# A linear-attention and FFN kernel: another order of the first steps, other filler products, later second halves of the attention output

## The chip, the cores and the metric

One core of one Trainium2 chip runs the whole program. The metric is the device time of one execution in microseconds (us); lower is better. TensorE is called PE here (PEld is its loading of the stationary operand), VectorE DVE, ScalarE ACT, GpSimd POOL; SyncE (SP) only issues DMAs.

## The reference: what is computed

Two stages, all in fp32 (the FFN's weights arrive in a wider format and are converted on the chip):

```python
for t in range(S):        # batch 4, heads 8, S = 768, head size 48
    state = alpha[:, :, t, :, None] * state + einsum('bhd,bhe->bhde', k[:, :, t], v[:, :, t])
    y[:, :, t] = einsum('bhd,bhde->bhe', q[:, :, t], state)
x = y.transpose(0, 2, 1, 3).reshape(3072, 384)
h = maximum(x @ w_in, 0)          # w_in 384 x 2048
out = (h * h) @ w_out             # w_out 2048 x 384
```

So every token gets a gated linear-attention output, and the outputs of all heads, side by side, go through a feed-forward network with a squared ReLU.

## The kernel before, in words

**Blocks.** The sequence of each batch is cut into six chunks of 128 tokens; a block is one chunk of one batch with all eight heads, so there are 24 blocks, numbered so that blocks 0 to 3 are the first chunks of the four batches. The state goes from block n to block n + 4.

**One block.** `load` (L130) brings alpha ("a"), q, k and v. `ln` takes the logarithm of alpha on ACT (L261); `cs` sums it along the tokens by one product with a triangle of ones on PE (L283, two PE rows); `eb` and `ei` take the exponential of the sum and of its negative on ACT (L294, L298); `mq` and `mk` scale q and k by them on DVE (L302). `qT` and `kT` turn them on PE (L354, four transposes each), `qc` and `kc` copy the results out of PSUM (L368). `sc` forms the scores (L413) and `kv` the sums of k times v (L442), 32 PE rows each. `am` masks the scores on DVE (L424), `us` adds the old state (L456), `lt` turns the last row of the decay (L337, copied out by ACT as "last", L344), and `st` makes the next state (L477, L479).

**A pair of blocks.** The output y is formed for two blocks together. `ga` (L502) does the scores and sums of the block n coming next, then the state's part and the first half of y for the pair a before it; `gb` (L524) does the second half of y (the other halves of the masked scores, L393) and then the scores and sums of block n + 1. The two halves are apart because one writes other rows of the PSUM banks than the other. `ev` (L596; `ep` in the written order, L616) copies y out of PSUM into x, the FFN's transposed input, in up to twelve pieces on ACT or DVE.

**The FFN.** Blocks go through it in groups of four: 24 blocks are six groups (0 to 5). `ffn_in` (L909) does it plainly for group 0, one of 16 columns blocks j at a time: three products (two PE rows each), the ReLU on ACT (L925) and the square on ACT (L928). The first four j are done in halves of 256 tokens (`ha`, `hb`), since the first pair's x is there before the second's. From group 1 on each fp32 product is split into three of a rounded type (`in_x`, `in_y`, L726; `out_x`, `out_y`, L809), whose parts DVE and ACT make (L653, L648, L701).

**Weights.** `weights` (L146) loads a slab, one eighth of w_in or w_out; `first` (L169) converts half of its bits on ACT (two rows, L179), `second` (L184) does the rest on DVE (four rows, L192 to L199).

**What sets the order.** The program is recorded under a manual schedule: each engine runs its instructions in the order written. Three things write it. (1) The prelude: `AT["pre"]` names the first loads, then fills (memsets), masks and a few products of zeros (`warm`, L236) are issued. (2) For blocks 0 to 3 a string, `AT["first"]`, is a list of words (step name and block), run one after the other. (3) After that `attention` (L1006) puts the same steps at planned times ("FFN steps", one being one unit of FFN work) and `weave` (L1051) mixes them with the FFN's units; `AT["ga"]` and `AT["gb"]` are the times of `ga` and `gb` after an attention pair's start.

**Loads.** All DMAs stand in one queue on SP in the order of issue. `move` (L108) makes a load wait until an earlier one has landed, about three loads back, so that the queue isn't filled far ahead:

```python
for before, took in reversed(under_way):
    if ahead >= AT["thrp" if us == 1.0 else "thr"]:
        tc.add_manual_dep(ins, before.name, ...)
        break
    ahead += took
```

**Names the prediction uses.** "Sums 2" is `cs2`, "scores 2" `sc2`, "log 2" `ln2`, and so on with the block's number; "slab 0" is the first eighth of w_in; a PE "row" is one line of the trace's records, of which an fp32 product has two.

Of the kernel before, what the change touches and what calls it, by code (L numbers as in the profile page):

```python
# [9 lines left out]
FP32 = mybir.dt.float32  # L10
FP32R = mybir.dt.float32r
# [4 lines left out]
AF = mybir.ActivationFunctionType  # L16
ALU = mybir.AluOpType
# [1 line left out]


GB = 4
AT = {'thrp': 4.5, 'cvo': 3.35, 'thr': 2.25, 'm48': 16, 'cvs': 3.9, 'cv1': 0.125, 'later': (0, 0, 4, 6, 0, 1, 0), 'evs': 0.1, 'lead': 4, 'post': 3, 'w_first': (46.0, 38.0, 49.0), 'wstep': 1.0, 'w_in_at': 2.5, 'w_in_by': 3.6, 'room1': 22, 'room': 24, 's0': 4, 'ahead': 6, 'late': 2, 'xs': 0.0, 'g0': ((0.5, 4, False, True, 27.75), (25.75, 6, True, True), (29.25, 8, True, False)), 'sc0': (3.25, 2.35, 2.35), 'g1': ((5.5, 8, False, 15.0), (13.0, 10, True), (35.25, 12, True)), 'g': ((2.075, 6, True), (14.25, 8, True)), 'g1x': 51.0, 'gx': 48.75, 'g0x': 56.25, 'k0': 2, 'h0': 15, 'k1': 4, 'h1': 3, 'h1by': 2, 'evs0': 0.7, 'tp': 'ADMD', 'tp1': 'ADAD', 'split': 8, 'o0': (46.5, 48.5), 'o1': (), 'o2': (21.25, 24.75, 24.5, 40.0, 35.25, 28.25), 'str1': 21.5, 'ga': 9.75, 'gb': 12.5, 'cv0': -1.25, 'pre': '1a 0a 0q 0k 1k 1q', 'cp': ('q2a', 'k2b', 'k0a', 'k3a', 'k3b', 'k0b', 'q0b', 'q3b', 'q2b', 'q3a'), 'evd': ((0, 0, 0), (0, 0, 1), (0, 1, 2), (0, 1, 3), (2, 0, 3), (2, 1, 1), (2, 1, 2)), 'first': 'ln0 load1v cs0 ei0 eb0 zeros4 mk0 mq0 qT0 kT0 ln1 cs1 kc0 ei1 warm0 load0v eb1 mk1 qc0 weights0 lt1 sc0 load2a mq1 load2q kT1 kc1 qT1 load2k load3a qc1 load3k kv0 am0 first0 load3v sc1 ln2 kv1 load3q us0 am1 weights6 us1 cs2 ya0 ei2 second0 eb2 lt0 ln3 yb0 load2v mq2 qT2 mk2 load4a ep00 ep01 qc2 kT2 cs3 kc2 eb3 ei3 zeros1 sc2 ep02 mq3 mk3 kT3 ep03 weights2 first1 st0 ha0 second1 lt2 kv2 am2 qT3 load4k kc3 qc3 ha1 weights5 first2 sc3 kv3 am3 load4q us2 ha2 us3 ya2 yb2 weights3 ep20 ep21 ep22 load4v ep23 second2 first3 weights1 st1 weights4 ha3 lt3 hb0 st2 second3 hb2 hb3 hb1 st3'}


RUN = {0: 128, 32: 32, 64: 64, 96: 32}
# [3 lines left out]
def kernel(  # L29
# [12 lines left out]
    nc = tc.nc  # L42
    B, H, S, D = q.shape
    C = 128
    NCH = S // C
    NP = H // 2
# [24 lines left out]
    s_t = [s_all.pop(0) for _ in range(B)]  # L71
    NV = 4
# [4 lines left out]
    for t in tiles["q"] + tiles["k"]:  # L77
        nc.gpsimd.memset(t[:, :, D:64], 0.0)

    NW = 8  # L80
    wt_pool = ctx.enter_context(tc.tile_pool(name="wt", bufs=26))
# [15 lines left out]
    lent = {("a", n): flat(wt("a_lent"))[:, 0 : H * D] for n in (2, 3)}  # L97
    for x, n in (("q", 2), ("q", 3), ("k", 3)):
        t = lent[x, n] = two_k("qk_lent", shape=(H, 64))
        nc.gpsimd.memset(t[:, :, D:64], 0.0)  # L100

    def tile_of(x, n):
        return lent.get((x, n), tiles[x][n % len(tiles[x])])
# [4 lines left out]
    def move(us, out, in_):  # L108
        ins = nc.sync.dma_start(out=out, in_=in_).ins
# [90 lines left out]

    for word in AT["pre"].split():
        load(int(word[0]), word[1:])
# [12 lines left out]
    ident = consts.tile([128, 128], FP32, name="ident")  # L215
    make_identity(nc, ident)
    causal = cv_pool.tile([128, C], FP32, tag="upper", name="causal")
    make_upper_triangular(nc, causal, 1.0, diag=True)
    causal_r = consts.tile([128, C], FP32R, name="causal_r")
    nc.gpsimd.tensor_copy(out=causal_r, in_=causal)  # L220
# [4 lines left out]
    for t in s_all + u_all:  # L225
# [10 lines left out]
    def warm(_):  # L236
        nc.tensor.matmul(
            out=ps_att.tile([128, NP, 64], FP32, tag="att", name="warm"),
            lhsT=s_t[0].rearrange("a p d -> a (p d)")[:, 0:128], rhs=s_t[0], start=True, stop=True,
        )  # L240

    for _ in range(3):
        warm(0)


# [18 lines left out]

    SPLIT = AT["split"]

# [106 lines left out]
    def kc(n):  # L373
        (copied if n < GB else turned_copied)("k", n)


    def zeros(n):

# [85 lines left out]
    def rows_of(n):  # L464
        return [slice(0, D), slice(64, 64 + D)] if n >= AT["m48"] else [slice(0, 128)]

# [174 lines left out]
    here, todo, room = {}, [], [22]  # L641
# [8 lines left out]
    late = [False]  # L650
# [83 lines left out]
    def in_x(j):  # L734
        acc["h", j] = ps_ffn.tile([128, GB * C], FP32, tag="att", name="h")
        in_passes(j, "b", "a", True, False)
        in_passes(j, "l", "l", False, True)
        x = acc["h", j]
        if kinds[0][j % 4] == "D":
            hid[j] = two_k("hid")  # L740
            nc.scalar.activation(out=hid[j], in_=x, func=AF.Copy, scale=E)  # L741
        else:
            nc.scalar.activation(out=x, in_=x, func=AF.Copy, scale=1.0 + E)  # L743

    def in_y(j):
        given.add(("hy", j))
        in_passes(j, "d", "d", False, True)
        if kinds[0][j % 4] == "D":
            combine(((hid[j], acc.pop(("h", j)), ALU.add, hid[j]),))

    kinds = [""]

    def in_post(j):
        need(("hy", j))
        given.add(("h", j))
        if kinds[0][j % 4] == "D":
# [7 lines left out]
        if kinds[0][j % 4] == "M":  # L764
# [144 lines left out]
    def ffn_in(g, j, cols=slice(0, GB * C)):  # L909
        need(("w", j * NW // NJ))  # L910
        if cols.start == 0:
            need(("x", 0))
        if cols.stop == GB * C:
            need(("x", 2))
        w, c0 = w_in[j * NW // NJ], j % (NJ // NW) * 128
        n = cols.stop - cols.start
        ps = ps_ffn.tile([128, GB * C], FP32, tag="att", name="h")[:, 0:n]
        for kk in range(KM):
            nc.tensor.matmul(  # L919
                out=ps, lhsT=w[:, kk, c0 : c0 + 128], rhs=xT[g][kk][:, cols],  # L920
                start=(kk == 0), stop=(kk == KM - 1),
            )
# [31 lines left out]
    steps = {f.__name__: f for f in (ln, sp, cs, eb, ei, mq, mk, bl, br, lt, qT, qc, kT, kc, ev)}  # L954
# [11 lines left out]

    steps["ep"] = ep
    steps["zeros"] = zeros

    def half_in(x, j):  # L970
        given.add(("h" + x, j))
# [5 lines left out]
    first = AT["first"]  # L977
    for word in first.split():
        f = max((x for x in steps if word.startswith(x)), key=len)
        rest = word[len(f) :]  # L980
        steps[f](*([int(rest[0]), rest[1:]] if f == "load" else map(int, rest)))


    PLAN = (
# [122 lines left out]
    cv0 = AT["cv0"]  # L1107
    cvs = AT["cvs"]
# [17 lines left out]
    for g in range(1, NG):  # L1126
# [11 lines left out]
        if g == 1:  # L1138
# [5 lines left out]
            n = min(AT["k0"], AT["k1"])  # L1144
# [34 lines left out]
```

## Time and profile before

| | |
|---|---|
| median of 3 runs | 518.98 us (518.58 to 520.09) |
| span of the profiled execution | 518.6 us |
| time of the profiled execution itself | the page gives its span alone |
| PE busy | 507.8 us (98%) |
| DVE busy | 355.7 us (69%) |
| ACT busy | 306.4 us (59%) |
| DMA moved | 102.34 MB, 197 GB/s in the mean |
| products of h in group 0 (L919) | 128x512: 0.43 us from start to start |

A busy PE is counted from an instruction's start to its modelled end, and products overlap, so what counts is the time from one start to the next. A line of the timeline gives start, length, engine, source line, operation, output and inputs, the number of instructions merged and, in brackets, how long the engine stood idle before and what ended that. The chain of waits goes backwards from the last instruction: at each step to what released it. The granted clock is 1.00 in all five-microsecond stretches up to 45 us.

### The profile page before, as it was taken

The numbers are of one execution on the slowest core, as the hardware profiler recorded it, in microseconds if no ns is written. First come the engines' busy times: TensorE is split into PE (matmuls) and PEld (weight loads), VectorE is DVE, ScalarE is ACT, GpSimd is POOL, SyncE is SP. The second block draws the span as 40 slices with busy tenths as digits, with TensorE's granted clock in tenths as the row PEclk, the third lists the DMA queues.
The fourth block names the chain that finished last, engine by engine and source line by source line (L and its number), as shares of the span: only waits on it lengthen the run. The fifth ranks groups of instructions, "written<-read, shape, count | busy, mean of one in ns | idle before, by whom it ended". The sixth has DMA issues, their size and how long they took to land.

```text
span 518.6 us, 13019 instructions
## 1 busy us (share of the span) xinstructions
PE 507.8 (98%) x5338; PEld 418.9 (81%) x5338; DVE 355.7 (69%) x628; ACT 306.4 (59%) x649; POOL 5.3 (1%) x29
## 2 busy tenths in 40 slices
PE   7899999999999999999999999999999999999997
PEld 5675455678888669987899988899988899988997
DVE  2766669986887877776697468587465487363861
ACT  4788898547888653485664276772275673164620
POOL 4000000000000000000000000000000000000000
PEclk9999999999999999999999999999999999999999
DMA  9999779472777786898884688864683545699201
GB/s 183 204 267 237 197 189 235 93 228 80 238 190 184 246 243 162 265 279 227 205 225 143 222 247 222 223 200 152 213 274 124 185 121 154 207 380 322 65 2 61
DMA packets 139323, 102.34 MB, mean 197 GB/s; under 512 B 109808, under 2 KB 115968, under 8 KB 139264
## 3 DMA queue, kind: packets, MB, share of 16 engines
q1 hardware_dynamic: 139264, 101.51, 68.2%
q8 instruction: 42, 0.69, 0.6%
q14 instruction: 17, 0.14, 0.1%
HBM read 84.16 MB, written 17.33 MB: 196 GB/s over the span
## 4 chain that ended last, share of the span: by engine, by line
PE 93%; DVE 4%; issue 1%; POOL 1%; ACT 1%; DVEq 0%; POOLq 0%
PE o L809 39%; PE h L726 32%; PE h L919 8%; PE y L393 4%; PE sckv L413 2%; PE T L578 2%; PE sckv L442 2%; PE cs L283 1%; PE cs L286 1%; DVE x L616 1%; PE cs L287 1%; DVE hd L648 1%; DVE hx L653 0%; DVE am L424 0%; ACT x L616 0%
## 5 line engine op out<-in xcount | busy, mean ns | idle before, releaser
L726 PE MATMUL h<-xd,wd 128*128 128x512 f32 x240 | 68.1, 396 | 1.1 <-issue 1.1
L726 PE MATMUL h<-xa,wb 128*128 128x512 f32 x240 | 68.7, 394 | 0.0
L726 PE MATMUL h<-xl,wl 128*128 128x512 f32 x240 | 67.9, 391 | 0.0
L648 DVE TENSOR_TENSOR hid<-h,hid 128x512 f32<-128x512 f32 x40 | 27.6, 689 | 51.1 <-PE h L726 51.0
L616 ACT COPY x<-y 48x256 f32<-48x256 f32 (+3 forms) x133 | 46.7, 365 | 21.2 <-PE y L393 18.8
L809 PE MATMUL o<-wb,ha 128*128 128x384 f32 x160 | 54.5, 340 | 0.0
L743 ACT ACTIVATE h<-h 128x512 f32<-128x512 f32 x40 | 23.3, 582 | 52.3 <-PE h L726 52.3
L809 PE MATMUL o<-wl,hl 128*128 128x384 f32 x160 | 53.7, 336 | 0.1
L809 PE MATMUL o<-wd,hd 128*128 128x384 f32 x304 | 53.7, 334 | 0.0
L809 PE MATMUL o<-w_out,hid 128*128 128x384 f32 x160 | 53.6, 489 | 0.0
L726 PEld LDWEIGHTS h<-xl,wl 128*128 128x128 f32 x240 | 45.1, 188 | 10.1 <-DVE xl L653 0.4
L809 PEld LDWEIGHTS o<-wd,hd 128*128 128x128 f32 x304 | 52.8, 188 | 0.0
L726 PEld LDWEIGHTS h<-xa,wb 128*128 128x128 f32 x240 | 44.4, 188 | 9.8 <-ACT hid L763 0.4
L726 PEld LDWEIGHTS h<-xd,wd 128*128 128x128 f32 x240 | 44.0, 188 | 9.1
L809 PE MATMUL o<-wb,hx 128*128 128x384 f32 x144 | 48.3, 336 | 0.0
L809 PE MATMUL o<-wl,hx 128*128 128x384 f32 x144 | 48.1, 334 | 0.0
L809 PEld LDWEIGHTS o<-w_out,hid 128*128 128x128 f32 x160 | 30.0, 190 | 19.7
L741 ACT ACTIVATE hid<-h 128x512 f32<-128x512 f32 x40 | 24.2, 606 | 32.9 <-PE h L726 32.5
L919 PE MATMUL h<-x,w_in 128*128 128x512 f32 (+1 forms) x120 | 43.4, 512 | 0.2 <-DVE x L616 0.2
L701 ACT ACTIVATE ha<-hid 128x512 fp32r<-128x512 f32 x40 | 25.1, 642 | 20.3 <-PE o L809 7.9
L919 PEld LDWEIGHTS h<-x,w_in 128*128 128x128 f32 x120 | 22.1, 190 | 17.8 <-issue 15.3
L653 DVE SCALAR_TENSOR_TENSOR hl<-ha,hid 128x512 fp32r<-128x512 f32 x40 | 27.5, 687 | 6.9 <-ACT ha L701 6.8
(111 smaller groups left out, 852.5 us busy)
## 6 DMA issues: line engine op xcount, KB each, us to landing
wd<-do SPq DMA_DIRECT2D x36, 384.0 KB
wl<-lo SPq DMA_DIRECT2D x34, 384.0 KB
wl<-li SPq DMA_DIRECT2D x32, 384.0 KB
wd<-di SPq DMA_DIRECT2D x32, 384.0 KB
raw<-in_moe_w_out_dram SPq DMA_DIRECT2D x8, 767.5 KB
raw<-in_moe_w_in_dram SPq DMA_DIRECT2D x8, 767.2 KB
v_in<-in_v_dram SPq DMA_DIRECT2D x24, 192.0 KB
out_dram<-osb SPq DMA_DIRECT2D x24, 192.0 KB
```

What stands on the lines that cost most here:

```text
L393: ins = nc.tensor.matmul(out=ys[e][64 * half : 64 * half + D + G * e, m % 2, p // 2, t], lhsT=lhsT, rhs=rhs, start=(half, e) not in seen, ...
L413: nc.tensor.matmul(out=ps[e][HALF[h], 0, p, :], lhsT=ks[rows, p, HALF[h]], rhs=qs[rows, p, HALF[h]], start=True, stop=True, skip_group_che ...
L442: nc.tensor.matmul(out=ps[h][64 * e : 64 * e + m, 1, p, G:64], lhsT=tile_of("k", n)[HALF[h], 2 * p + e, 0:m], rhs=tiles["v"][n % NV][HALF[ ...
L616: copy(out=x[kk][to : to + m, t : t + 2], in_=blk[n]["y"][e][r : r + m, :, p // 2],)
L648: nc.vector.tensor_tensor(out=o, in0=x, in1=z, op=op)
L653: nc.vector.scalar_tensor_tensor(out=o, in0=x, scalar=c, in1=y, op0=ALU.mult, op1=op)
L701: nc.scalar.activation(out=a, in_=x, func=AF.Copy, scale=NEAR * E)
L726: nc.tensor.matmul(out=acc["h", j], lhsT=here[w, "i", p][:, kk, jj * 128 : (jj + 1) * 128], rhs=x_parts[x][:, kk], start=start and kk == 0 ...
L741: nc.scalar.activation(out=hid[j], in_=x, func=AF.Copy, scale=E)
L743: nc.scalar.activation(out=x, in_=x, func=AF.Copy, scale=1.0 + E)
L809: nc.tensor.matmul(out=acc[t][:, 0:DM], lhsT=lhs[:, t * C : (t + 1) * C], rhs=rhs, start=start, stop=stop, skip_group_check=True,)
L919: nc.tensor.matmul(out=ps, lhsT=w[:, kk, c0 : c0 + 128], rhs=xT[g][kk][:, cols], start=(kk == 0), stop=(kk == KM - 1),)
```

## The change

It touches tables and the prelude; the FFN from group 1 on is the same work.

- The first loads and their order: k of block 1 comes third, ahead of q and k of block 0. In the written order the first slab of weights goes ahead of both v loads, alpha of block 3 goes ahead of k and q of block 2, the second slab goes ahead of k3, v3 and v2.
- POOL makes the triangle of ones first; DVE fills the padding of the q and k tiles, which POOL did; the states s0 to s2 are filled later.
- Products of zeros: two of 512 columns at the start instead of three of 256; in the written order one product of 128 columns at two places, instead of four of 128, one of 256 and one of 128.
- The words of `AT["first"]` are in another order: the sums of block 1 directly behind those of block 0; the copies of k1, k2 and q1 out of PSUM on DVE (before, the names in `AT["cp"]` matched no block and all copies were on ACT); other pieces of x on DVE (`evd`).
- Squares of `ffn_in` named in `AT["hv"]` are done on DVE: four of 256 columns and that of j = 4 with 512.
- `AT["gb"]` goes from 12.5 to 14.0, so that in the planned part the second half of a pair's y, the copies into x, the scores of the pair's second block and three loads come 1.5 FFN steps later.

```diff
-AT = {... 'gb': 12.5, 'pre': '1a 0a 0q 0k 1k 1q',
- 'cp': ('q2a', 'k2b', 'k0a', 'k3a', ...),
- 'evd': ((0,0,0), (0,0,1), (0,1,2), (0,1,3), (2,0,3), (2,1,1), (2,1,2)),
- 'first': 'ln0 load1v cs0 ei0 eb0 zeros4 mk0 mq0 qT0 kT0 ln1 cs1 kc0 ei1 warm0 load0v eb1 mk1 qc0
-  weights0 lt1 sc0 load2a mq1 load2q kT1 kc1 qT1 load2k load3a qc1 load3k kv0 am0 first0 load3v sc1
-  ln2 kv1 load3q us0 am1 weights6 us1 cs2 ya0 ei2 second0 eb2 lt0 ln3 yb0 load2v mq2 qT2 mk2 load4a
-  ep00 ep01 qc2 kT2 cs3 kc2 eb3 ei3 zeros1 sc2 ep02 mq3 mk3 kT3 ep03 weights2 first1 st0 ha0 second1 ...'}
+AT = {'warms': 0, 'wides': 2, 'hv': ((1,256), (2,256), (3,0), (3,256), (4,0), (4,256)),
+ ... 'gb': 14.0, 'pre': '1a 0a 1k 0q 0k 1q', 'cp': ('k1', 'k2', 'q1'),
+ 'evd': ((0,0,0), (0,0,1), (0,0,3), (2,0,0), (2,0,1), (2,1,3)),
+ 'first': 'ln0 cs0 ln1 cs1 weights1 load0v ei0 eb0 mq0 load1v load2a ei1 qT0 zeros1 mk1 load3a mk0
+  kT0 eb1 kT1 mq1 qc0 load2k kc0 sc0 load2q first0 lt1 qT1 kc1 am0 kv0 qc1 us0 ln2 sc1 kv1 load3q
+  cs2 am1 us1 eb2 ei2 ln3 lt0 weights6 load3k second0 ya0 yb0 cs3 load3v mq2 mk2 ep00 load2v weights0
+  eb3 mq3 ep01 ei3 kT2 kc2 qT2 load4a qc2 zeros1 ep02 st0 qT3 ep03 sc2 mk3 first1 ha0 kT3 am2 ...'}
...
-    for t in s_all[0:B]:
-        nc.gpsimd.memset(t, 0.0)
     s_t = [s_all.pop(0) for _ in range(B)]
+    nc.gpsimd.memset(s_t[3], 0.0)
+    causal = ...; make_upper_triangular(...); causal_r = ...; ident = ...
...
+    for t in pads:
+        nc.vector.memset(t[:, :, D:64], 0.0)
...
-    for _ in range(3):
+    for _ in range(AT["wides"]):
+        nc.tensor.matmul(
+            out=ps_att.tile([128, 2 * NP, 64], FP32, tag="att", name="warm"),
+            lhsT=s_t[3].rearrange("a p d -> a (p d)")[:, 0:128],
+            rhs=s_t[3][:, 0:1, :].to_broadcast([128, 2 * NP, 64]), start=True, stop=True,
+        )
+    for _ in range(AT["warms"]):
         warm(0)
...
-        nc.scalar.activation(out=hid[j][:, cols], in_=r, func=AF.Square)
+        if (j, cols.start) in AT["hv"]:
+            nc.vector.tensor_tensor(out=hid[j][:, cols], in0=r, in1=r, op=ALU.mult)
+        else:
+            nc.scalar.activation(out=hid[j][:, cols], in_=r, func=AF.Square)
```

More of the change, by code (lines that the diff above doesn't have):

```diff
@@ new lines @@
+AT = {'warms': 0, 'wides': 2, 'hv': ((1, 256), (2, 256), (3, 0), (3, 256), (4, 0), (4, 256)), 'thrp': 4.5, 'cvo': 3.35, 'thr': 2.25, 'm48': 16, 'cvs': 3.9, 'cv1': 0.125, 'later': (0, 0, 4, 6, 0, 1, 0), 'evs': 0.1, 'lead': 4, 'post': 3, 'w_first': (46.0, 38.0, 49.0), 'wstep': 1.0, 'w_in_at': 2.5, 'w_in_by': 3.6, 'room1': 22, 'room': 24, 's0': 4, 'ahead': 6, 'late': 2, 'xs': 0.0, 'g0': ((0.5, 4, False, True, 27.75), (25.75, 6, True, True), (29.25, 8, True, False)), 'sc0': (3.25, 2.35, 2.35), 'g1': ((5.5, 8, False, 15.0), (13.0, 10, True), (35.25, 12, True)), 'g': ((2.075, 6, True), (14.25, 8, True)), 'g1x': 51.0, 'gx': 48.75, 'g0x': 56.25, 'k0': 2, 'h0': 15, 'k1': 4, 'h1': 3, 'h1by': 2, 'evs0': 0.7, 'tp': 'ADMD', 'tp1': 'ADAD', 'split': 8, 'o0': (46.5, 48.5), 'o1': (), 'o2': (21.25, 24.75, 24.5, 40.0, 35.25, 28.25), 'str1': 21.5, 'ga': 9.75, 'gb': 14.0, 'cv0': -1.25, 'pre': '1a 0a 1k 0q 0k 1q', 'cp': ('k1', 'k2', 'q1'), 'evd': ((0, 0, 0), (0, 0, 1), (0, 0, 3), (2, 0, 0), (2, 0, 1), (2, 1, 3)), 'first': 'ln0 cs0 ln1 cs1 weights1 load0v ei0 eb0 mq0 load1v load2a ei1 qT0 zeros1 mk1 load3a mk0 kT0 eb1 kT1 mq1 qc0 load2k kc0 sc0 load2q first0 lt1 qT1 kc1 am0 kv0 qc1 us0 ln2 sc1 kv1 load3q cs2 am1 us1 eb2 ei2 ln3 lt0 weights6 load3k second0 ya0 yb0 cs3 load3v mq2 mk2 ep00 load2v weights0 eb3 mq3 ep01 ei3 kT2 kc2 qT2 load4a qc2 zeros1 ep02 st0 qT3 ep03 sc2 mk3 first1 ha0 kT3 am2 kc3 second1 qc3 ha1 weights5 lt3 kv2 us2 load4k sc3 kv3 first2 ha2 am3 weights4 us3 st1 ya2 load4v yb2 ep20 ep21 lt2 weights3 ep22 ep23 ha3 second2 st3 hb2 first3 hb3 hb0 second3 hb1 load4q st2 weights2'}
@@ L68 @@
     u_all = kept("us", 3, [128, NP, 64])
-    for t in s_all[0:B]:
-        nc.gpsimd.memset(t, 0.0)
     s_t = [s_all.pop(0) for _ in range(B)]
+    nc.gpsimd.memset(s_t[3], 0.0)
+    causal = cv_pool.tile([128, C], FP32, tag="upper", name="causal")
+    make_upper_triangular(nc, causal, 1.0, diag=True)
+    causal_r = consts.tile([128, C], FP32R, name="causal_r")
+    nc.gpsimd.tensor_copy(out=causal_r, in_=causal)
+    ident = consts.tile([128, 128], FP32, name="ident")
+    make_identity(nc, ident)
     NV = 4
@@ L76 @@
     }
-    for t in tiles["q"] + tiles["k"]:
-        nc.gpsimd.memset(t[:, :, D:64], 0.0)
+    pads = tiles["q"] + tiles["k"]
     NW = 8
@@ L99 @@
         t = lent[x, n] = two_k("qk_lent", shape=(H, 64))
-        nc.gpsimd.memset(t[:, :, D:64], 0.0)
+        pads.append(t)
     def tile_of(x, n):
@@ L214 @@
     nc.scalar.preload_act_table_set("natural_log_exp_and_others")
[L215 to L220, printed above, removed]
     halves_mask = consts.tile([128, C // 2], FP32, name="halves_mask")
@@ L224 @@
         nc.gpsimd.tensor_copy(out=halves_mask[rows], in_=causal[rows, rows])
-    for t in s_all + u_all:
+    for t in s_t[0:3] + u_all + s_all:
         nc.gpsimd.memset(t, 0.0)
@@ L238, in warm @@
             out=ps_att.tile([128, NP, 64], FP32, tag="att", name="warm"),
-            lhsT=s_t[0].rearrange("a p d -> a (p d)")[:, 0:128], rhs=s_t[0], start=True, stop=True,
+            lhsT=s_t[3].rearrange("a p d -> a (p d)")[:, 0:128], rhs=s_t[3], start=True, stop=True,
         )
-    for _ in range(3):
+    for _ in range(AT["wides"]):
[5 more added lines that the diff above has]
+    for _ in range(AT["warms"]):
         warm(0)
@@ L374, in kc, with wide, tiny @@
         (copied if n < GB else turned_copied)("k", n)
+    def wide(n):
+        ps = bank(n, "zeros", (2 * NP, 64))
+        for _ in range(n):
+            nc.tensor.matmul(
+                out=ps, lhsT=s_t[3].rearrange("a p d -> a (p d)")[:, 0:128],
+                rhs=s_t[3][:, 0:1, :].to_broadcast([128, 2 * NP, 64]), start=True, stop=True,
+            )
+    def tiny(n):
+        ps = bank(n, "zeros", (2 * NP, 64))
+        for _ in range(n):
+            nc.tensor.matmul(
+                out=ps[0:8, 0, 0:1], lhsT=s_t[3][:, 0, 0:8], rhs=s_t[3][:, 0, 0:1],
+                start=True, stop=True,
+            )
     def zeros(n):
@@ L738, in in_x @@
         x = acc["h", j]
-        if kinds[0][j % 4] == "D":
+        if kinds[0][j % len(kinds[0])] == "D":
             hid[j] = two_k("hid")
@@ L755, in in_post @@
         given.add(("h", j))
-        if kinds[0][j % 4] == "D":
+        if kinds[0][j % len(kinds[0])] == "D":
             h = hid[j]
@@ L968 @@
     steps["zeros"] = zeros
+    steps["tiny"] = tiny
+    steps["wide"] = wide
     def half_in(x, j):
@@ L980 @@
         rest = word[len(f) :]
-        steps[f](*([int(rest[0]), rest[1:]] if f == "load" else map(int, rest)))
+        steps[f](*([int(rest[0]), rest[1:]] if f == "load" else [int(rest)] if f in ("zeros", "tiny", "wide") else map(int, rest)))
     PLAN = (
```

5 lines of the change are left out of this document (2 added, 3 removed).

## The prediction

> **What bounds the kernel now.** I read the busy tenths of the span first, then five-microsecond stretches, then the waits and the timeline of the first 40 us. The tenths come first.
>
> ```profile
> PE   7899999999999999999999999999999999999997
> DVE  2766669986887877776697468587465487363861
> ACT  4788898547888653485664276772275673164620
> ```
>
> PE has slack only in the first two slices (0 to 26 us) and in the last. By stretches:
>
> ```profile
> 5.00:10.00 5.00, 4.33 (x15) 3.53 (x16) 1.03 (x2) 1.80 (x4) 1.19 (x6) 1.00 1.32 186
> ...
> 15.00:20.00 5.00, 3.90 (x169) 3.15 (x173) 4.67 (x10) 3.30 (x7) 0.00 (x0) 1.00 0.84 165
> 20.00:25.00 5.00, 3.64 (x73) 2.92 (x64) 4.83 (x12) 4.47 (x12) 0.00 (x0) 1.00 1.01 263
> ...
> 40.00:45.00 5.00, 5.00 (x17) 2.91 (x16) 4.69 (x10) 2.62 (x8) 0.00 (x0) 1.00 0.99 245
> ```
>
> After the length come busy PE, PEld, DVE, ACT, POOL, then clock, DMA share, GB/s. From 40 us PE is full, so what the change does early is worth as many us as it brings forward the moment from which PE never waits again. The chain of waits in time order has that moment:
>
> ```profile
> 36.10 0.42 DVE x L616
> 36.52 0.03 issue
> 36.55 0.44 DVE x L616
> 36.99 0.04 issue
> 37.04 8.02 PE h L919 x28
> ```
>
> The last copy into the first group's x ends at 36.99; the FFN's products start at 37.04 and run through. Where the time before that goes:
>
> ```profile
> 8.56 0.41 SPq L109 DMA_DIRECT2D raw<-in_moe_w_in_dram  x1
> 11.19 0.37 SPq L109 DMA_DIRECT2D a_lent<-in_alpha_dram  x1
> ...
> 16.67 0.53 ACT L261 ACTIVATE a_lent<-a_lent 128x384 f32<-128x384 f32 x1
> ...
> 20.11 0.52 ACT L261 ACTIVATE a_lent<-a_lent 128x384 f32<-128x384 f32 x1
> ```
>
> ACT takes the logarithm of block 2 only at 16.67, behind the conversion of the first weight slab (14.88 to 16.79), and that of block 3 at 20.11, behind the second copy of "last". Their cumulative sums follow at 17.25 and 21.66 on PE.
>
> **When the loads land.** The loads are one queue. I summed GB/s over half-microsecond stretches and took 0.197 MB for a load and 0.786 MB for a slab (192.0 and 767.2 KB in the page's last part): alpha of block 0 is complete at 4.0, the eighth load at 10.2, the first slab at 12.9, the second goes from 20.7 to 23.4. So a load takes 1.03 us and a slab 2.7. The log of block 0 starts at 5.04 and the load that waits for v0 issues at 11.19, so a landing is about 1.0 behind its bytes. In the new queue order (alpha 1, alpha 0, k1, q0, k0, q1, slab 0, v0, v1, alpha 2, alpha 3, k2, q2, q3, slab 1, k3, v3, v2, slab 2) that gives landings, as estimates from these rows: q1 9.2, slab 0 11.9, v0 12.9, v1 13.9, alpha 2 15.0, alpha 3 16.0, k2 17.0, q2 18.1, q3 19.1, slab 1 21.8, k3 22.8, v3 23.9, v2 24.9, slab 2 27.6. The other end: from 13.7 to 18.0 the queue of before needs 1.43 us for each of three loads (133 and 86 GB/s in 15 to 17), and its third slab takes 3.2. With 1.43 from v0 to q2 and 3.2 for slabs, k3 lands at 26 and v2 at 28.
>
> **The change, part by part.**
>
> *Products of zeros and fills.* Three products of 256 columns become two of 512 (four PE rows at 0.86 instead of six at 0.43: 1.10 to 4.6 instead of 3.7); four of 128 (1.71 us, 7.28 to 8.99) and one of 256 go; one of 128 is added before block 0's k transpose, at most 0.43. POOL makes the mask first (causal_r done near 2.0 instead of 4.29) and DVE fills the pads (eight of about 0.2, over before 5). Worth nothing: the first sums wait for ACT's log at 5.04 to 5.56, which waits for alpha 0, and that load keeps its place. Without this cover it would cost the 0.86 that PE runs longer.
>
> *Blocks 0 and 1.* The sums of block 1 go ahead of block 0's transposes, so its exponentials end near 9.5 instead of 12.06. But block 0's values now come after the slab, 12.9 instead of 11.2. Even with every product at the slow spacing (0.73 for half a sum), block 1's second transpose ends by 13.2 and its copy, now on DVE, by 13.9. That copy from PSUM has no DVE row: between 0.42 (256 columns) and 0.79 (a masked copy of 2x256) I take 0.65, nearest to 0.69 of the 512-column sum that reads PSUM. So this is a loss hidden by the next wait: sc1 13.95, kv1 to 15.05.
>
> *Block 2 and 3 gates.* Slab 0 lands at 11.9, ACT converts it to 13.85 (1.91), copies "last" to 14.2, and takes log 2 at its landing, 15.0. Sums 2 run at 15.6 against 17.25; the y products of blocks 0 and 1 at 16.7 to 18.6 against 18.09 to 20.3; log 3 comes ahead of "last" at 17.2 and sums 3 run at 18.6 against 21.66. This is the gain: 1.65 at y, 3.0 at sums 3.
>
> *Where part of it is given back.* DVE is full here (4.67 and 4.83 of 5). Converting slab 0 takes it 15.8 to 18.75 (2.93, as in 17.18 to 20.11); then q2, k2 (0.55 each), a copy of x 0.42, q3 0.55 to 20.8, two copies, the copy of k2's transpose (0.65, new on DVE) to 22.2. So scores 2 start at 22.25 against 22.80: only 0.55 left. Then the state (0.72), two copies of x, k3 to 24.3. PE: first half-width FFN unit 22.9 to 24.4 (its last third waits for x), k3 transposes 25.0, second unit 26.4, "last" of block 3 0.45, kv2 27.3, scores 3 (copies ready 26.7) 27.95, kv3 28.4, third unit 29.9 (its weights 28.0), y of blocks 2 and 3 to 31.7 against 33.75. The x copies there took 33.75 to 36.99, 3.24; the new split is as long. End near 35.0: **2.0 earlier**. With late loads the same walk has k3 scaled at 26.6, kv2 at 29.5, y to 33.9, end 37.2: **0.2 later**. The 1.03 row holds for most loads, so I take 1.7.
>
> *Squares moved to DVE* (four of 256 columns, 0.42 each on ACT, and one of 512, 0.63): after 35 us PE is full with four half units (1.46 each) and needs the third slab's weights only behind these, near 41; DVE has them at about 38.7. Nothing; if later than 41, what is missing.
>
> *Second half of y 1.5 steps later.* No work changes: 8 to 16 o products or nine h products (1.4 to 2.8 us) go ahead of it. The tightest place is the end of group 1: y moves from 204.1 to 206.9, its twelve ACT copies (4.37) end at 211.9 instead of 209.2, the three splits' first parts at 213.6, the DVE parts at 214.5; PE wants them at 214.08 to 215.2, each in time by 0.3 or more. The v and k loads move with it and have 8 steps left. One stall may go or come:
>
> ```profile
> 237.35 0.62 PE L726 MATMUL h<-xd,wd 128*128 128x512 f32 x2
> 239.08 0.40 PE L726 MATMUL h<-xd,wd 128*128 128x512 f32 x1 [1.11 <-issue]
> ```
>
> It stands between two dense bursts of attention rows and waits for no engine. Bounds: -1.1 if wider spacing removes it, +1.1 if another appears; I take 0, since the nearest row, this one, already holds one.
>
> **Sum.** 1.7 off a span of 518.6 is 516.9. The page gives the profiled execution as that span and no time around it; the median of the three runs is 0.38 above it. The same 1.7 off 518.98 gives **517.3**. About 0.3%, 1.56 us, is what a measurement here can tell from no change, so faster means under 517.4 and slower over 520.5.
>
> **Rivals.**
> (a) *Loads late.* The slab ahead of v0 and the second ahead of k3, v3, v2 make these the gates. For it: the 1.43 stretch. Against: that stretch follows one issue of 2.34 us, which the new order may not have. 0.2 later: 519.2.
> (b) *PE stays at the slow spacing.* Transposes start 0.21 apart until 9.62 and 0.11 apart from 10.02, after PE had been busy since 5.67; the granted clock says 1.00 in both, so only spacing shows it. The new order has no zeros to fill the time from sums 1 to the transposes. If the switch comes only with the products after 13.3, some 4.2 us of PE work there runs at half speed, 2.1 lost, of which the wait for log 2 hides 0.7: 1.7 - 1.4 = 0.3 gained, 518.7. For it: 1.10 to 4.03 busy did not switch. Against: PE is nearly unbroken from 5.6 to 10 again.
> [...]
> (c) *Slower: DVE of the later steps lands in front of a split.* In group 2 the chain stays on DVE from 256.72 to 271.42, and gb's block there takes 2.86 (267.79 to 270.65) with PE waiting 0.1. An out step of eight products is 1.4. If the moved block falls ahead of a split that PE needs next, PE stands 2.86 - 1.4 = 1.46 in each of groups 2, 3 and 4: 4.4 lost, 1.7 gained, 521.7. It decides once DVE is behind by more than one step. Against: groups 3 and 4 show no wait at all.
> (d) *Larger gain.* 1.7 and the stall of 1.11: 516.2.
>
> **How the numbers follow.** Forecast 0.47 (gain 1.0 to 2.0, of which 0.38 under 517.4), (a) 0.18, (b) 0.10, (c) 0.15, (d) 0.10. Faster 0.38 + 0.10 = 0.48; same 0.09 + 0.18 + 0.10 = 0.37; slower 0.15. The range leaves out (c) and little else: from 515.6, (d) with 0.6 of DMA luck or the 2.0 end, to 519.6, (a) with one more 0.4 of queue.
>
> **What would show it.** Right: log 2 near 15.0, sums 3 near 18.6, scores 2 near 22.3, last x copy near 35. Wrong: v0 past 14 or k3 past 25 (a); products over 0.4 apart at 14 us (b); PE waiting for hl or hx after 200 us (c).

## The result, and the profile after

The changed kernel takes **521.37 us** (median of 8 runs, 519.81 to 526.33) against 518.54 for the kernel before on the same chip (8 runs): a ratio of 1.0061, 95% interval 1.0034 to 1.0089. It is slower by 0.6%, outside the forecast range and on the other side. The profiled execution took 520.53 us, 0.84 under the median, with a span of 518.8: in the runs that have both, a time is the span plus 1.7 to 1.9.

Line numbers of the new kernel are higher: L943 is the half-width h product (L919 before), L750 the split h product (L726), L640 the x copy (L616), L417 y (L393), L267 the logarithm (L261).

The busy tenths of the new kernel, on its page:

```profile
PE   7899999999999999989999999999999999999997
DVE  5867669976987876676697468687465496363861
ACT  4776996556877661675773175863275783164620
```

PE has a new 8 in the 18th slice (220 to 233 us) and no other sign of a loss. The stages show more. First come the early five-microsecond stretches (same columns as before):

```profile
5.00:10.00 5.00, 2.97 (x15) 1.96 (x16) 1.87 (x4) 3.16 (x7) 0.09 (x2) 1.00 1.25 233
...
15.00:20.00 5.00, 4.45 (x121) 3.10 (x122) 4.89 (x10) 3.19 (x10) 0.00 (x0) 1.00 0.82 184
20.00:25.00 5.00, 4.25 (x56) 3.40 (x55) 4.67 (x12) 4.51 (x10) 0.00 (x0) 1.00 1.03 242
```

From 5 to 10 us PE does 1.4 us less (the zeros are gone), from 15 to 25 it does 1.2 more. On ACT the logarithms of blocks 2 and 3 come 2.3 and 3.2 us earlier than at 16.67 and 20.11:

```profile
14.39 0.52 ACT L267 ACTIVATE a_lent<-a_lent 128x384 f32<-128x384 f32 x1 [0.64 <-DMA a_lent<-in_alpha_dram]
...
16.89 0.52 ACT L267 ACTIVATE a_lent<-a_lent 128x384 f32<-128x384 f32 x1
```

and in the chain of waits the FFN's run starts at 35.05 instead of 37.04. **The start is 1.99 earlier, as worked out.** One landmark can be followed through all traces: the first turn of each pair of blocks (T, L602 or L578), from the timelines of PE, in us.

| kernel | T 1 | T 5 | T 6 | T 7 | T 8 | T 9 | T 10 | span |
|---|---|---|---|---|---|---|---|---|
| before | 66.02 | 193.05 | 227.22 | 250.12 | 308.09 | 329.59 | 386.99 | 518.6 |
| changed | 64.03 | 191.25 | 227.21 | 249.58 | 307.53 | 329.84 | 387.24 | 518.8 |
| 1: new start, y at 12.5 | 63.72 | 191.03 | 225.16 | 247.08 | 305.06 | 326.56 | 383.96 | 515.5 |
| 4: one pair at 12.5 | 64.61 | 192.37 | 226.50 | 248.88 | 306.83 | 329.12 | 386.52 | 518.0 |
| 5: loads still later | 70.39 | 197.43 | 231.61 | 253.97 | 311.95 | 334.22 | 391.63 | 523.1 |
| 8: three pairs at 12.5 | 64.36 | 191.41 | 225.54 | 247.61 | 305.58 | 327.09 | 384.50 | 516.0 |

The lead of 2.0 at T 1 is 1.8 at T 5 and nothing at T 6: **1.8 is lost before 227** (loss A). From T 6 to T 7 the changed kernel takes 22.37, where the first experiment takes 21.92 (B; the 22.90 of before hold its stall of 1.11); from T 8 to T 9 it takes 22.31 against 21.50 (C). Behind T 9 all take the same.

Loss A on PE, then on SP's queue, in the timelines of the changed kernel (wd and wl are loaded parts of the split weights, here of w_in; osb is a piece of the result on its way out):

```profile
222.94 0.93 PE L750 MATMUL h<-xd,wd 128*128 128x512 f32 x3 [1.56 <-ACT ha L725]
```

```profile
215.05 1.31 SPq L113 DMA_DIRECT2D out_dram<-osb  x3
216.47 0.40 SPq L113 DMA_DIRECT2D v_in<-in_v_dram  x1
216.96 0.67 SPq L113 DMA_DIRECT2D out_dram<-osb  x1
217.69 0.42 SPq L113 DMA_DIRECT2D wd<-di  x1
218.16 0.45 SPq L113 DMA_DIRECT2D wl<-li  x1
221.49 0.38 SPq L113 DMA_DIRECT2D k_in<-in_k_dram  x1
221.99 0.51 SPq L113 DMA_DIRECT2D wd<-di  x1
```

The waits of SP between 214 and 224 (total, times, longest):

```profile
SPq L113 <- DVE osb L672: 6.6, 1, 6.6
SPq L113 <- DMA v_in<-in_v_dram: 2.8, 1, 2.8
```

The releaser that is named for PE's 1.56 (ACT's ha, which ends at 222.93) is not what PE needed: in the fifth experiment the same product starts at 227.43, while ACT is still in a step three ahead of this ha (the hid of L787, to 227.46). What ended the wait is the wd issued at 217.69. The profile's view of tile wd gives it 5.1 us from issue to landing, so it landed at 222.80, 0.14 before PE starts. The wd issued at 221.99 can't be it: the DMA moves 128 GB/s from 222 to 223, which is 128 KB, and a wd has 384 KB.

So the wd that PE needs stands behind v. The later v now comes in the middle of the stores, which wait for DVE's osb, and directly ahead of the last store and this wd. Before, v was issued at 210.36, ahead of the stores, and the wd (215.96) had only the four stores just ahead of it. `move` then holds k for 2.8 until v has landed, but k stands behind this wd; what it delays are later parts, and PE never stands for those.

### The profile page after: what moved, and what is told of

It is laid out like the page before. It is cut to its first block, busy times and chain, and to the rows that moved or that the text cites. A ratio compares the mean times of both kernels' runs of the same rounds, so it can differ in the third digit from the quotient of the medians.

```text
span 518.8 us, 13008 instructions
## 1 busy us (share of the span) xinstructions
PE 507.1 (98%) x5328; PEld 415.6 (80%) x5328; DVE 360.3 (69%) x642; ACT 304.6 (59%) x643; POOL 4.2 (1%) x21
## 4 chain that ended last, share of the span: by engine, by line
PE 90%; DVE 4%; ACT 3%; DMA 1%; issue 1%; SPq 1%; DVEq 0%; ACTq 0%; POOLq 0%
PE o L833 39%; PE h L750 31%; PE h L943 8%; PE y L417 4%; PE sckv L437 2%; PE T L602 2%; PE sckv L466 2%; ACT x L640 1%; DMA k_in<-in_k_dram 1%; DVE hd L672 1%; SPq L113 1%; DVE am L448 1%; PE cs L289 0%; DVE hx L677 0%; PE cs L292 0%
## 5 line engine op out<-in xcount | busy, mean ns | idle before, releaser
L750 PE MATMUL h<-xd,wd 128*128 128x512 f32 x240 | 68.1, 396 | 1.6 <-ACT ha L725 1.6
L750 PE MATMUL h<-xa,wb 128*128 128x512 f32 x240 | 68.8, 394 | 0.5 <-ACT x L640 0.5
L750 PE MATMUL h<-xl,wl 128*128 128x512 f32 x240 | 67.9, 391 | 0.0
L640 ACT COPY x<-y 32x256 f32<-32x256 f32 (+2 forms) x135 | 48.2, 366 | 24.3 <-PE y L417 22.2
L750 PEld LDWEIGHTS h<-xl,wl 128*128 128x128 f32 x240 | 45.1, 188 | 10.0 <-DVE xl L677 0.4
L750 PEld LDWEIGHTS h<-xa,wb 128*128 128x128 f32 x240 | 44.4, 188 | 10.6 <-ACT x L640 1.3
L750 PEld LDWEIGHTS h<-xd,wd 128*128 128x128 f32 x240 | 44.0, 188 | 11.0 <-ACT h L767 2.0
L943 PE MATMUL h<-x,w_in 128*128 128x512 f32 (+1 forms) x120 | 43.4, 513 | 0.3 <-ACT x L640 0.3
L943 PEld LDWEIGHTS h<-x,w_in 128*128 128x128 f32 x120 | 22.1, 190 | 18.3 <-issue 15.1
```

The source lines that it names most:

```text
L640: copy(out=x[kk][to : to + m, t : t + 2], in_=blk[n]["y"][e][r : r + m, :, p // 2],)
L750: nc.tensor.matmul(out=acc["h", j], lhsT=here[w, "i", p][:, kk, jj * 128 : (jj + 1) * 128], rhs=x_parts[x][:, kk], start=start and kk == 0 ...
L943: nc.tensor.matmul(out=ps, lhsT=w[:, kk, c0 : c0 + 128], rhs=xT[g][kk][:, cols], start=(kk == 0), stop=(kk == KM - 1),)
```

## The experiments

Each kernel was compared with runs of the kernel before on the same chip. "Low clock" counts the runs whose granted clock, averaged over the span, was under 0.998; "full" is the median of the others. Experiments 1 to 4, 5 to 8, 9 to 12 and 13 to 15 each shared a chip's runs of before (medians 519.34, 519.20, 519.53, 519.37; low clock 10 of 108).

| experiment | median | ratio, 95% interval | low clock | full |
|---|---|---|---|---|
| 1 new start, y at 12.5 | 518.22 | 0.9983 (0.9963 to 1.0003) | 3 of 12 | 517.72 |
| 2 old start, y at 14.0 | 522.10 | 1.0050 (1.0033 to 1.0067) | 1 of 8 | 522.04 |
| 3 loads at old time | 521.90 | 1.0041 (1.0016 to 1.0067) | 7 of 12 | 519.41 |
| 4 one pair at 12.5 | 519.77 | 1.0016 (0.9996 to 1.0037) | 3 of 12 | 519.53 |
| 5 loads still later | 519.41 | 1.0004 (0.9993 to 1.0015) | 1 of 12 | 519.34 |
| 6 as 1, old zeros | 518.26 | 0.9978 (0.9965 to 0.9991) | 0 of 11 | 518.26 |
| 7 as 1, squares on ACT | 518.32 | 0.9987 (0.9970 to 1.0004) | 1 of 12 | 518.10 |
| 8 three pairs at 12.5 | 518.10 | 0.9996 (0.9972 to 1.0020) | 4 of 12 | 517.37 |
| 9 as 4, next sums later | 529.63 | 1.0184 (1.0142 to 1.0226) | 6 of 6 | none |
| 10 as 8, rows shifted | 524.20 | 1.0086 (1.0064 to 1.0107) | 4 of 6 | 522.35 |
| 11 as 8, slabs later | 518.22 | 0.9974 (0.9960 to 0.9987) | 0 of 11 | 518.22 |
| 12 as 8, old zeros | 517.91 | 0.9971 (0.9960 to 0.9982) | 0 of 7 | 517.91 |
| 13 as 4, copies together | 520.68 | 1.0045 (1.0018 to 1.0072) | 4 of 12 | 520.32 |
| 14 before, rows shifted | 525.25 | 1.0115 (1.0087 to 1.0144) | 1 of 6 | 525.07 |
| 15 as 12, slabs later | 518.37 | 0.9974 (0.9958 to 0.9991) | 0 of 12 | 518.37 |

The theory: the start gains 2.0, the later y loses more at three places. The main rival: something in the new start harms the later work.

**1 and 2: each part alone.**

```diff
-AT = {... 'gb': 14.0, ...}    # experiment 1, in the changed kernel
+AT = {... 'gb': 12.5, ...}
-AT = {... 'gb': 12.5, ...}    # experiment 2, in the kernel before
+AT = {... 'gb': 14.0, ...}
```

> The changed kernel, with the second half of y back at 12.5 steps: the new start alone. Theory (the new start gains the 1.99 that the end of the last x copy shows, 35.00 against 36.99, and the moved y loses more than that): 518.5 - 2.0 = 516.5, faster than before by 0.4%. Rival (the loss comes from what the new start does to later work, the squares on DVE or the weights' order): 518.5 or more, and a wait near 222.9 in the profile still.

> The kernel before, with the second half of y at 14.0 steps: the later y alone. Theory: the changed kernel is 2.8 over before, and its start gains 2.0, so this move alone costs 4.8: 523.3, slower by 0.9%. Rival (the move is harmless without the new start): 518.5 to 519.

Measured: 518.22 (517.72 at full clock, 1.6 under before) and 522.10 (522.04, 2.7 over). The signs are as expected, the sizes smaller than the forecast 2.0 and 4.8. In the first the lead is 2.0 to 2.3 at every T up to T 6 and no wait near 222.9 is left; the second has it (1.19 before 224.62, "DMA wd<-di"; this wd landed at 224.48, again 0.14 ahead). So the two parts are opposite in sign, and A, B and C come with the moved y alone. The rival falls for these three. But the parts add up to +1.1 and the changed kernel shows +2.6 at full clock; that difference is taken up below. Not expected: a quarter of the first's runs have a low clock.

**3, 4 and 5: loss A.**

```diff
-'later': (0, 0, 4, 6, 0, 1, 0)
+'later': (0, 0, 2.5, 4.5, 0, 1, 0)      # experiment 3
+'later': (0, 0, 5.5, 7.5, 0, 1, 0)      # experiment 5
...
+                if f == "gb" and n0 == 12:   # experiment 4
+                    w = t + 12.5
```

> The changed kernel, in which y stays at 14.0 steps but the later v and k loads are back at their old times (2.5 and 4.5 steps behind it instead of 4 and 6). PE, DVE, ACT and POOL have the same instructions in the same order; only SP's queue differs. Theory (the v load behind the stores holds k and the weight parts back at the start of group 2): the wait of 1.56 before 222.9 goes and the lead of 2.0 at 227 is kept, 521.4 - 2.0 = 519.4. Rival (the later y itself and its ACT copies make the whole loss): 521.4, no change against the changed kernel.

> The changed kernel, with y at 12.5 steps for one pair only, the one that ends group 1 (its y stood at 204.1 before). All other pairs keep 14.0. Theory: the loss at the start of group 2 goes (2.0), those of groups 2 and 3 stay: 519.4. Rival (the loss is made in groups 2 to 4 alone, the wait near 222.9 is an accident of this profile): 521.4.

> The changed kernel with its second v and k loads another 1.5 steps later (5.5 and 7.5 behind y). PE, DVE, ACT and POOL unchanged; in SP's queue the v load falls behind all four stores and one wd, wl pair, and the k load behind the third wd. Theory (it is the k load, waiting for v's landing in front of the third wd part, that makes PE wait before 222.9): with the third wd now ahead of k the wait of 1.56 goes although the loads are later; T of group 2 near 225.3 and about 2 below the changed kernel, near 519.5. Rival (v and k simply land too late): the wait grows by the 1.5 steps, some 2.1, to 3.7, and the time to 523 or more.

Measured at full clock: 519.41, 519.53 and 519.34, which is 1.6 to 1.8 below the changed kernel (521.13, or 2.6 over before, on its own chip). In all three the wait is gone from the traces. The fifth tells the most: its loads are the latest of all, and it is as fast as with the earliest. Its queue, from the timeline of SP:

```profile
221.27 1.82 SPq L113 DMA_DIRECT2D out_dram<-osb  x4
223.14 0.45 SPq L113 DMA_DIRECT2D wd<-di  x1
...
224.19 0.38 SPq L113 DMA_DIRECT2D v_in<-in_v_dram  x1
```

The wd that PE needs next (223.14) is now issued ahead of v (k comes at 229.79), and PE starts its product at 227.43 without a wait. In the fourth, where v stands ahead of the stores, the same wd takes 3.4 us from issue to landing; with v in front of it, it took 5.1 (changed kernel) and 4.7 (second experiment). So it is not the lateness of v or k that costs, but v's place in front of this wd. The expectation of the fifth named the k load in front of a later wd instead. The run's time fits that theory as well; the landing at 222.80 does not. The median over all runs of the third (521.90) missed the forecast by 2.5, since 7 of its 12 runs had a low clock.

**8: everything that the later y costs is at three places.**

```diff
+                if f == "gb" and n0 in (12, 14, 18):
+                    w = t + 12.5
```

> The changed kernel with y at 12.5 steps for three pairs only: the one that ends group 1 and the first of groups 2 and 3. The other seven keep 14.0. Theory (all that the later y costs is lost at these three places: a start of T in group 2 of 1.6 to 2, 0.5 near 245 and 0.7 near 324): as fast as the first experiment, 517.7, and no PE wait of 0.4 or more behind 40 us that names an engine. Rival (the cost is spread over all pairs): between 517.7 and 519.5.

Measured: 517.37 at full clock (517.7 forecast), and no wait of 0.12 or more that names an engine behind 40 us; seven pairs keep the later y at no cost. The median of all runs is 518.10, with 4 of 12 at a low clock.

**9 and 13: what B and C are.** In the changed kernel, the timelines of ACT and then PE:

```profile
240.92 3.32 ACT L640 COPY x<-y 32x256 f32<-32x256 f32 x9 [0.74 <-PE y L417]
244.25 0.60 ACT L765 ACTIVATE hid<-h 128x512 f32<-128x512 f32 x1
244.86 1.15 ACT L640 COPY x<-y 64x256 f32<-64x256 f32 x3
```

```profile
245.27 0.96 PE L750 MATMUL h<-xa,wb 128*128 128x512 f32 x3 [0.50 <-ACT x L640]
```

PE's three products wait for the first of the last three copies (244.86 + 0.38 = 245.24). The cumulative sums of the next pair come 0.7 steps behind the moved y, 2.2 before.

```diff
-'g': ((2.075, 6, True), (14.25, 8, True))    # experiment 9, with n0 in (12, 16, 20, 24) at 12.5
+'g': ((2.075, 6, True), (15.75, 8, True))
-'evs': 0.1                                   # experiment 13
+'evs': 0.0
```

> As the fourth experiment (the pair that ends group 1 at 12.5 steps), but in groups 2 to 4 the second pair of each group is moved 1.5 steps later as a whole, with its own y at 12.5 steps: each y stands where it stood, at 14.0 after the first pair's start and at the same step for the second, but the next pair's cumulative sums follow the first pair's y at 2.2 steps again instead of 0.7. Theory (the waits near 245 and 324 come from the sums that follow y too closely, so that PSUM banks still wait for nine x copies in a row on ACT): both waits go, the stretches from T to T are 21.9 and 21.5 instead of 22.4 and 22.3, and at full clock the time is 519.5 - 1.2 = 518.3. Rival (the later y by itself delays the h products' banks, whatever follows): 519.5 with a wait of 0.4 or more near 245.

> As the fourth experiment, with the spacing of the four parts of the x copies at 0.0 steps instead of 0.1: the last three copies of a pair then go ahead of the conversion of an h on ACT (0.60) instead of behind it. PE, DVE and POOL have the same instructions in the same order; ACT the same in another order. Theory (PSUM banks held by the row of copies on ACT make the waits near 245 and 324): the wait near 245 falls from 0.48 to 0.1 or less, the stretch from T to T in group 2 from 22.4 to 22.0, and the time at full clock from 519.5 to 519.0. Rival (the banks come free anyway, PE waits for the h on ACT or for DVE): 0.48 or more again, or a wait of about 0.5 in another place.

The ninth is a failed experiment: the waits near 245 and 324 are gone, but the moved pair, squeezed against its own y, makes others (2.37 before 264.40 and 1.59 before 347.99, for DVE's us and am), and 529.63 tells nothing of B's price. The thirteenth came out larger and with the opposite sign: +0.8 at full clock instead of -0.5. PE has the same order, and now the sums wait:

```profile
246.06 0.45 PE L292 MATMUL cs<-hi,causal_r 128*128 128x384 f32 x1 [1.17 <-ACT x L640]
```

ACT's twelve copies run in one row from 242.43 to 246.78, and the sums start at the end of the tenth. So B's cause is confirmed (whoever gets y's PSUM tile next, of eight in the program's one pool, waits for the row of copies) but not my idea that a shorter row must help: with the copies recorded ahead of the sums, the sums got the tile that the h products had got, one step sooner. That the choice of tile follows the order in which work is recorded is argued from these two traces, not shown by itself. C is less clear: near 324 the changed kernel's four sums start 0.25 to 0.52 apart (0.18 in the first experiment), and the one wait listed there, 0.18, names DVE's s, which reads another tile. That C has B's cause is argued.

**6 and 7: what was priced at nothing.**

```diff
-'warms': 0, 'wides': 2, ... mq0 load1v load2a ei1 qT0 zeros1 mk1 ...    # 6
+'warms': 3, 'wides': 0, ... zeros4 mq0 load1v load2a ei1 qT0 mk1 ...
-'hv': ((1, 256), (2, 256), (3, 0), (3, 256), (4, 0), (4, 256))          # 7
+'hv': ()
```

> The new start with y at 12.5 steps as in the first experiment, but with the products of zeros of before: three of 256 columns, then four of 128 behind block 0's exponentials, none before block 0's k transpose. Theory (the products of zeros are worth nothing, the first sums wait for ACT): the same as the first experiment, 517.7, and the prelude's end at 35.0. Rival 1 (they bring PE to its fast spacing earlier): the sums of blocks 0 and 1 at 0.73 instead of 0.38 for a half, up to 2.1 slower. Rival 2 (the wide products raise the chance of a granted clock under 0.998: 15 of 44 runs with the new start so far, 3 of 39 with the old): one run in ten, instead of one in three, under 0.998, and a median nearer to 517.5.

> The new start with y at 12.5 steps as in the first experiment, but with all squares of the first half-width FFN units back on ACT. Theory (moving them was worth nothing, PE is full behind 35 us): the same as the first experiment, 517.7 within 0.3. Rival (they matter for the x copies that end at 35.0): 0.5 to 1 slower, and the last x copy later than 35.5.

Measured: 518.26 and 518.32 against 518.22: nothing, in all three medians. At full clock they are 0.5 and 0.4 over the first, which these runs can't tell from no change. Rival 1 of the sixth falls: the sums of blocks 0 and 1 take 1.53 for four rows with the new zeros (changed kernel) as with the old (sixth). They are not always so fast: in the traces of the ninth (new zeros) and the fifteenth (old zeros) these rows start 0.64 to 0.77 apart. Rival 2 looked right (0 of 11), and led to the next group.

**10, 11, 12 and 14: the low clocks.** The fifth's profile caught one. PE's timeline, then two one-microsecond stretches behind it (granted clock third from the end):

```profile
29.61 0.33 PE L417 MATMUL y<-qs,us 48*48 48x64 f32 x7
32.48 0.91 PE L417 MATMUL y<-qs,us 48*64 48x64 f32 x24 [2.54 <-issue]
```

```profile
32.00:33.00 1.00, 0.52 (x20) 0.52 (x24) 0.00 (x0) 0.00 (x0) 0.00 (x0) 0.56 0.83 279
33.00:34.00 1.00, 1.00 (x48) 1.00 (x41) 0.00 (x0) 0.00 (x0) 0.00 (x0) 0.50 1.00 357
```

PE stands 2.54 with no releaser but "issue", and then runs at half clock (0.50) until 42.4; the mean over the span is 0.990. The third, seventh and thirteenth have the same stall in the same place (1.99, 1.46, 2.26; the last with half clock for 3.4). Counting PE and PEld rows up to each stall of this kind in all traces gives 442, 946, 2718, 3727, 5497 to 5499, 6259 and 8023 to 8025: from the first, 0, 2, 9, 13, 20, 23 and 30 times 252.8. The stall of 1.11 that before shows at 237.97 (row 5499) is one of them. I call 252.8 rows a block and a stall at its boundary a late block: that PE gets its rows in blocks is my reading of these counts. The changed kernel's 10,656 rows stand beside this line of the DMA queues (packets, MB, share):

```profile
q8 instruction: 42, 0.69, 0.5%
```

That is one packet of 16 KB for 253.7 rows, near the 252.8 between the stalls. That these packets bring PE its rows, and that a stall of up to 2.62 us (tenth experiment) is one that comes late, is my estimate from the two numbers; no trace shows it, nor that this queue serves PE alone.

Row 946 lies 7 products into y of blocks 2 and 3. In the changed kernel PE gets there 4.1 us after row 694 (25.5 to 29.6), in the kernel before 5.1 (25.7 to 30.8), outside a burst. With the old products of zeros in the new start (sixth) it is 4.8, and outside the burst too.

```diff
-... weights1 load0v ei0 eb0 mq0 load1v ...           # experiment 10; in 14 tiny12 stands ahead of zeros4
+... weights1 load0v ei0 eb0 tiny12 mq0 load1v ...
-... ha1 weights5 lt3 ... am3 weights4 us3 st1 ya2 load4v yb2 ep20 ...      # 11
+... ha1 lt3 ... am3 us3 st1 ya2 load4v yb2 weights5 weights4 ep20 ...
```

> As the eighth experiment, with 12 products of one column (24 rows with their weight loads) added behind block 0's exponentials, where PE idles about 1.0 anyway. They move every later PE row by 24 places. Theory (PE's rows come in blocks of about 252; a block boundary at row 946 lies 7 products into the y of blocks 2 and 3, only 4.0 us behind the boundary at row 694, and when the next block comes late there PE stands 1.5 to 2.5 and the clock may fall to half for 3.4 to 10 us): with the boundary now 24 rows earlier, 5.2 us behind the one before it and ahead of the burst, at most 1 run in 12 shows a clock under 0.998 (4 of 12 in the eighth experiment), and the median over all runs is that of the full-clock runs there, 517.4. Rival (the low clocks have another cause, such as the wide products of zeros): 3 or 4 runs in 12 again.

> As the eighth experiment, with the loads of two weight slabs (issued at 25.1 and 30.1) moved behind the y of blocks 2 and 3. PE, DVE, ACT and POOL have the same instructions in the same order and PE's block boundaries are where they were. Theory (the block that PE waits for at row 946 is itself a transfer, late because the load queue's slabs fill the DMA engines at 0.9 to 1.1 from 25 to 30): at most 1 run in 12 under 0.998. Rival (the wait has nothing to do with the DMA traffic): 3 or 4 runs in 12. The slabs land some 5 us later, needed from 37 us on: 0 to 1 lost in both cases.

> As the eighth experiment, with the old products of zeros of the sixth (four more products, so PE's rows are 8 later, and the boundary at row 946 lies about 4.9 us behind the one before it instead of 4.0). Theory: no more than 1 run in 12 under 0.998, as in the sixth (0 of 11), and a median of 518, within 0.3 of the sixth. Rival (the sixth had luck): 3 or 4 runs in 12.

> The kernel before with 12 products of one column added ahead of its four products of zeros: 24 more PE rows, nothing else. Theory (late blocks follow the number of rows alone): the boundary at row 5497 falls into the first y near 236, as in the tenth experiment, which stood 2.6 there and 1.3 near 341 in its profile; most runs 3 to 6 over the kernel before, 522.5 to 525, with clocks under 0.998 in a third of them or more. Rival (the tenth experiment's stalls come from the new start or from the moved y): 519.5 plus at most 0.5.

The tenth missed its forecast of 517.4 by 6.8, and yet it speaks for the theory. Its 24 rows did take the stall near 30 away (0.35 is left, at row 948). But they moved row 5497 from the second y of a pair (0.23 lost there in the eighth) into the first, and row 8023 from the o products into the y near 341:

```profile
233.38 0.68 PE L417 MATMUL y<-am,v_in 64*48 64x64 f32 x27
236.68 0.33 PE L417 MATMUL y<-am,v_in 64*48 64x64 f32 x4 [2.62 <-issue]
```

with 1.29 at the second place and half clock from 237.7 to 241.2. The forecast had weighed one boundary of 42. The fourteenth does the same to the kernel before: 525.25, 5.9 over it, with stalls of 0.86, 1.37, 1.20 and 1.20 at rows 2718, 5499, 6259 and 8025. So the new start is not needed for it, only the count of rows; my forecast of its low clocks (a third) was too high, 1 of 6. The eleventh leaves every PE row where it was and moves two slabs: 0 of 11 low, against 4 of 12 in the eighth, so the load traffic looks like part of the cause. The twelfth has the old zeros, as the sixth, on the eighth: 0 of 7. With the boundary eased in one of these two ways, none of 41 runs (6, 11, 12, 15) had a low clock; with it in the burst at full traffic (the changed kernel, 1, 3, 4, 5, 7, 8, 13), 25 of 92. The kernel before had 10 of 108.

**15: both remedies.**

> The twelfth experiment (old products of zeros, the new start, y at 12.5 steps for three pairs and 14.0 for the others) with the two weight slabs behind the burst as in the eleventh. Theory: two remedies for the same late block do not add up: 517.5 to 518.2, no run under 0.998, faster than before by 0.3%. Rival (the slabs' later landing costs when it is not needed as a remedy): 518.5 or more.

Measured: 518.37, 0 of 12: they do not add up. **Four versions are faster than before with a whole interval under 1: the sixth, eleventh, twelfth and fifteenth.** The twelfth has the lowest median, 517.91 against 519.53, faster by 0.29% (0.18 to 0.40%); these runs can't tell the four apart. The changed kernel itself was not run on these chips.

## Why the prediction was wrong, point by point

- *Prelude.* Right nearly to the digit: log 2 14.39 (15.0 forecast), sums 3 at 18.19 (18.6), scores 2 at 22.00 (22.25), the copy of 512 columns from PSUM on DVE 0.69 (0.65 taken), the last x copy's end 35.00 (35.0). By itself this part gave 1.6 at full clock (1.7 taken).
- *Zeros, fills, squares: nothing.* Right (6 and 7), but for the row counts, which the prediction leaves out: four products fewer leave PE 4.1 us instead of 4.8 for one block.
- *Second half of y: nothing.* **The step that failed**, at "The v and k loads move with it and have 8 steps left". The time left to v and k was enough: no product waited for them. This step asks when the moved loads are needed and not what stands behind them. The later v comes in front of a wd that has no such time left: with v in front it took 5.1 us to land (3.4 in the fourth experiment, where v stands ahead of the stores); PE was ready for it at 221.38, and it landed at 222.80. That is 1.4 to 1.8 us (A). The tightest place for y itself was also looked for at the wrong end: the splits at 214 were in time, but at two later pairs PE stood (B, 0.5, for a PSUM tile that y's copies still read; C, 0.8, argued to be the same).
- *The stall of 1.11.* Priced at 0 of either sign; it is a late block and belongs to that execution. Before's median probably does not hold it: that execution's span of 518.6 means some 520.3 us, an estimate from the spans and times above, over every median of before. So the span was not 0.38 under the median but its execution about 1.3 over it, and rival (d) counted the stall as a gain that the median could hardly give.
- *Rivals.* (a) and (b) fall: the end of the prelude came on time, and in the changed kernel's trace the first sums ran at 0.38 a row. (c) named the right part and sign, 521.7 against 521.37, for a wrong reason: between 256 and 272 no PE wait is new. Its chance of 0.15 rested on DVE alone; a rival that priced the move's DMAs was missing.
- *The sum as it is.* Against before without its stall, the changed kernel's trace has -2.0 at T 1, +0.2 up to T 5, +1.8 (A), +0.6 (B) and +0.8 (C). That makes the +1.4 of T 10: 387.24 - (386.99 - 1.11). The median shows +2.6 at full clock and +2.8 over all. What is left, 1.2 to 1.5, stays open. Two things fit it. Late blocks of row 946 cost 1.46 to 2.54 in four profiles (in two of them with the clock still full), but the executions that make the median have no traces. And before took 518.54 on this chip but 519.20 to 519.53 on the four chips of the experiments.

## What to carry to other kernels

When a step moves, list its DMAs and read the queue as it will then stand: what is behind each, and how soon is that needed. A load that comes a little later can slip in front of weights that have nothing to do with it and make them late; coming later still, behind them, can cure it. Take the load that ended a wait from its time of landing, not from the time of issue or from the name that the profile gives: here both pointed elsewhere. And where a timeline has bursts of short products and stalls with "issue" alone, count the rows up to them: here 12 added products (24 rows) moved the stalls to other work, and the kernel before took 5.9 us more (fourteenth experiment).

## What the runs showed of the hardware

- The stalls of PE with "issue" as the only releaser, 0.2 to 2.6 us long, lie whole numbers of 252.8 rows apart (rows 442 to 8025), mostly in bursts of 64-column products; no trace has more than four of 0.8 or more at its 42 boundaries. What PE waits for there, and how far ahead that is asked for, was not found.
- The granted clock fell to 0.50 behind some idle stretches of PE and not behind others. Stalls of 2.26, 2.37, 2.54 and 2.62 us were followed by half clock, and so was one of 1.59 with another 0.32 right behind it (ninth experiment, before 347.99 and 348.60; half clock from 350.4 to 353.9). Stalls of 1.99 and 1.56 were not, so the length alone does not decide. Half clock lasted 3.4 us four times and 10 once. Runs show 0.997, 0.993 and 0.990 for the span, which is about 3, 7 and 10 us of half clock in 520. What decides when the clock falls, and for how long, was not found.
- The first sums ran at the fast spacing (1.53 us for four rows) from 5.1 us on at the earliest, after either set of zeros in most traces of the new start, though PE had idled 0.2 to 1.3 us before them; in two (the ninth and fifteenth) they were slow (0.64 to 0.77 from row to row), as in all three of the old start (0.77 and 0.64 in before). No run tells what decides it.
